# Set-up inside the fixed order, attention masks on GpSimd, new planner durations, a new copy order and dummy matmuls, in a fused attention and gated-convolution kernel

## The chip, the cores and the metric

The kernel runs on one core of a Trainium2 chip. The metric is the device time in microseconds (us) from the first to the last instruction of the run, as a median of several runs. A profiled run's *span* is a little shorter than the time quoted. A core has these engines: PE (matrix multiply, with weight loads shown as PEld), DVE (VectorE), ACT (ScalarE), POOL (GpSimd) and SP, which here issues most DMA transfers. SBUF and PSUM are the core's two on-chip memories; PE's results land in PSUM, and DVE or ACT copy them out to SBUF.

## The reference, cut to what matters

```python
# q, k, v: (8 batches, 8 heads, 576 positions, 64)
scores = (q @ k.T) / sqrt(64)
scores = where(abs(i - j) <= 32, scores, -1e9)       # window of 65 positions
x = softmax(scores) @ v                              # -> (8, 576, 512)
h = relu(x @ w_in)                                   # 512 -> 1024
gate = sigmoid(conv3(h))                             # 3 taps along the positions, per channel
out = (h * gate) @ w_out                             # 1024 -> 512
```

## The kernel before: the parts concerned

The kernel does not leave its order to a scheduler. Each piece of work is an `Op` with a believed duration on each engine that may run it. A list planner places all of them on a model of the engines and of PSUM's eight banks, and the instructions are emitted in the order of the planned starts. Every engine then runs its own list strictly in that order:

```python
def act(n): return ("ACT", 0.000833 * n + 0.068)          # believed us for n elements
def dve(n, mode=1): return ("DVE", n / (960.0 * mode) + 0.076)
...
with tc.manual_schedule():
    for op in plan.place():          # sorted by planned start
        op.run(op.eng)
```

The set-up (identity, band mask, zeroed paddings) stands ahead of that block and is placed by the framework. q and k come in as rows, 9 consecutive positions to a partition, and are transposed on PE, 4 + 4 + 1 position blocks at a time. The copy out of PSUM puts position `9*x + j` of head pair `g` in its place in `qT` or `kT`:

```python
o_ = T[:, :, ...].rearrange("p g (x j) -> p g x j", j=RP)       # RP = 9
def cp(e, o_=o_[:, :, :, j0:j1], a=a, n=n, sl=sl):              # n = j1 - j0 = 4 or 1
    copy(e, o_, ps(sl, 128 * a, 128 * (a + n)).rearrange(
        "p (j x g) -> p g x j", j=n, x=32))
on = dict([act(128 * n), dve(128 * n)])
```

The innermost index is `j`: four bf16 elements side by side in SBUF, then a step of nine. The masks multiply the exponentials on DVE:

```python
nc.vector.tensor_tensor(out=x, in0=x, in1=m__, op=ALU.mult)
```

The softmax here doesn't subtract the row's maximum and nothing guards it: scores larger than these inputs give would overflow.

## Time and profile before

The kernel before took 268.31 us (two runs, 267.78 to 268.85), and its profile spans 264.9 us. The main readings (busy time by stage, DVE's costly groups, the masks slowed beside POOL's casts, the waits of the set-up) are in the prediction below. Two more lines belong to the argument. The first is the engines' busy time in the whole span; the second, from the table by line and shape, is the group on ACT that copies `kT` (count, then busy us and mean ns of one, then idle time of the engine just before).

```profile
PE 226.6 (86%) x2515; PEld 137.7 (52%) x2538; DVE 201.0 (76%) x459; ACT 180.3 (68%) x367; POOL 77.0 (29%) x103
```

```profile
L247 ACT CAST kT<-ps_all 128x512 bf16<-128x512 f32 x29 | 20.2, 743 | 1.8 <-PE ps_all L451 1.4
```

In whole, the q and k copies of 512 elements are 64: 29 on DVE and 35 on ACT. The *own time* of an instruction is its end less the end of the one before it on its engine, so that the overlap of neighbours is taken off.

| before | us |
|---|---|
| time, median | 268.31 |
| 512-element q/k copy, own time (mean), DVE / ACT | 0.64 / 0.66 |
| 128-element q/k copy, own time (mean), DVE | 0.61 |

### The profile page before, as it was taken

To read this page: it belongs to the slowest core of one execution; us is meant where nothing else is said; L and a number is where in the kernel's file an instruction comes from. 1 tells how busy PE (TensorE), PEld (TensorE's weight loads), DVE (VectorE), ACT (ScalarE), POOL (GpSimd) and SP (SyncE) were. 2 spreads that over 40 slices of the span, in tenths; PEclk is the share of its full clock that TensorE was granted. 3 is DMA by queue.
4 is the path that set the end of the run, shared out by engine and by line. 5 is a ranking of instruction groups with operands and counts; after the bars stand their busy time and mean duration, and the time that the engine had idled before them with its cause. 6 is when DMAs were issued, how large, how long until landed. Compare 5 with 4: busy or idle time off the path is not lost.

```text
span 264.9 us, 6661 instructions
## 1 busy us (share of the span) xinstructions
PE 226.6 (86%) x2515; PEld 137.7 (52%) x2538; DVE 201.0 (76%) x459; ACT 180.3 (68%) x367; POOL 77.0 (29%) x103
## 2 busy tenths in 40 slices
PE   0337867995779998899999999999999999999973
PEld 0225757684367555455546555555464555555531
DVE  5452595369688999998888989899898998757650
ACT  2874877689357577768675858686867595666641
POOL 2677696319225506401224123231200000000000
PEclk9999997999799999999999999999999999999999
DMA  5999999999979898999999898952213131311113
GB/s 178 272 354 255 334 313 251 281 289 259 268 223 235 159 169 246 177 321 316 193 223 301 126 266 179 270 132 62 59 42 92 40 83 60 112 58 61 66 55 119
DMA packets 71123, 49.65 MB, mean 187 GB/s; under 512 B 54428, under 2 KB 54452, under 8 KB 71092
## 3 DMA queue, kind: packets, MB, share of 16 engines
q1 hardware_dynamic: 71056, 49.22, 74.3%
q8 instruction: 20, 0.33, 0.6%
q14 instruction: 11, 0.09, 0.1%
q10 hardware_dynamic: 36, 0.01, 0.0%
HBM read 32.52 MB, written 9.44 MB: 158 GB/s over the span
## 4 chain that ended last, share of the span: by engine, by line
PE 69%; DVE 17%; ACT 7%; issue 2%; DMA 2%; SPq 1%; POOL 1%; ACTq 0%; DVEq 0%
PE ps_all L680 24%; PE ps_all L752 22%; PE ps_all L710 12%; PE ps_all L549 5%; DVE attn L530 5%; DVE qT L253 4%; PE ps_all L451 3%; PE ps_all L502 3%; ACT kT L247 2%; ACT attn L515 2%; DMA kst<-in_k_dram 2%; DVE gT L732 2%; DVE xn L569 2%; DVE ps_all L725 2%; DVE kT L253 1%
## 5 line engine op out<-in xcount | busy, mean ns | idle before, releaser
L680 PE MATMUL ps_all<-xT,w_in_sb 128*128 128x385 bf16 (+4 forms) x448 | 81.1, 314 | 3.3 <-DVE xT L253 1.5
L752 PE MATMUL ps_all<-w_out_sb,gT 128*128 128x512 bf16 x265 | 66.8, 384 | 5.1 <-DVE gT L732 3.0
L732 DVE SCALAR_TENSOR_TENSOR gT<-ps_all,hT 128x384 bf16<-128x384 f32 (+3 forms) x112 | 55.1, 502 | 12.2 <-ACT ps_all L729 11.1
L729 ACT ACTIVATE ps_all<-ps_all 128x384 f32<-128x384 f32 (+3 forms) x112 | 49.2, 445 | 21.7 <-DVE ps_all L725 14.6
L725 DVE SCALAR_TENSOR_TENSOR ps_all<-hT,conv_w_sb,ps_all 128x384 f32<-128x384 bf16 x80 | 49.2, 624 | 15.9 <-PE ps_all L710 15.3
L696 ACT ACTIVATE hT<-ps_all 128x385 bf16<-128x385 f32 (+4 forms) x112 | 49.4, 452 | 14.8 <-PE ps_all L680 13.8
L680 PEld LDWEIGHTS <-w_in_sb 128*128 128x128 bf16 x448 | 41.2, 101 | 24.5 <-issue 2.3
L710 PE MATMUL ps_all<-hT,diag_w 128*128 128x384 bf16 (+3 forms) x256 | 51.0, 303 | 1.1 <-ACT hT L696 1.1
L752 PEld LDWEIGHTS <-gT 128*128 128x128 bf16 x288 | 27.8, 99 | 34.6 <-issue 6.0
L763 ACT COPY y<-ps_all 128x512 f32<-128x512 f32 x36 | 21.2, 588 | 30.7 <-PE ps_all L752 26.6
L249 POOL TENSOR_SCALAR ve<-vst 128x512 bf16<-128x512 f32 (+1 forms) x39 | 25.0, 652 | 47.1 <-PE ps_all L549 28.2
L515 ACT ACTIVATE attn<-ps_all 128x1024 bf16<-128x1024 f32 (+1 forms) x40 | 36.7, 943 | 2.1 <-PE ps_all L502 1.8
L530 DVE TENSOR_TENSOR attn<-attn,mask 128x1024 bf16<-128x1024 bf16 (+1 forms) x48 | 31.8, 682 | 5.1 <-ACT attn L515 4.9
L249 POOL TENSOR_SCALAR qn<-qst 128x1152 bf16<-128x1152 f32 (+1 forms) x18 | 19.5, 1091 | 48.1 <-issue 18.0
L253 DVE CAST qT<-ps_all 128x512 bf16<-128x512 f32 (+1 forms) x41 | 29.5, 736 | 5.3 <-PE ps_all L451 5.0
L569 DVE TENSOR_TENSOR xn<-ps_all,rec 128x256 bf16<-128x256 f32 (+1 forms) x64 | 30.4, 487 | 0.6
L710 PEld LDWEIGHTS <-diag_w 128*128 128x128 bf16 x256 | 21.8, 101 | 10.9 <-issue 1.3
L247 ACT CAST kT<-ps_all 128x512 bf16<-128x512 f32 (+1 forms) x32 | 22.7, 752 | 2.1 <-PE ps_all L451 1.4
L549 PEld LDWEIGHTS <-attn 128*64 128x64 bf16 x640 | 14.9, 112 | 17.5 <-issue 12.4
L549 PE MATMUL ps_all<-ve,attn 128*64 128x65 bf16 x384 | 20.2, 200 | 3.4 <-DVE attn L530 2.1
L451 PE MATMUL ps_all<-ident,qn 128*128 128x128 bf16 x144 | 15.4, 230 | 8.0 <-ACT qn L247 6.4
L249 POOL TENSOR_SCALAR kn<-kst 128x1152 bf16<-128x1152 f32 (+1 forms) x19 | 19.1, 1006 | 7.8 <-DMA kst<-in_k_dram 5.0
(47 smaller groups left out, 155.0 us busy)
## 6 DMA issues: line engine op xcount, KB each, us to landing
qst<-in_q_dram SPq DMA_DIRECT2D x32, 288.0 KB, 4.6
kst<-in_k_dram SPq DMA_DIRECT2D x32, 288.0 KB, 5.2
out_dram<-y SPq DMA_DIRECT2D x36, 256.0 KB, 2.3
vst<-in_v_dram SPq DMA_DIRECT2D x23, 256.0 KB, 6.1
vo<-ve SPq DMA_DIRECT2D x28, 130.0 KB, 4.5
vst<-in_v_dram SPq DMA_DIRECT2D x16, 192.0 KB, 5.7
wst<-in_moe_w_in_dram SPq DMA_DIRECT2D x2, 1024.0 KB, 8.5
wst<-in_moe_w_out_dram SPq DMA_DIRECT2D x2, 1024.0 KB, 9.2
```

The lines of the kernel that those rows point to most:

```text
L249: nc.gpsimd.tensor_scalar(out=out_, in0=in_, scalar1=1.0, scalar2=0.0, op0=ALU.mult, op1=ALU.add)
L253: nc.vector.tensor_copy(out_, in_)
L515: add(act(2 * w), t + 0.1, lambda e: nc.scalar.activation(at, ps(sl, 0, 1024).rearrange("p (e x) -> p e x", e=2)[:, :, 0:w], AF.Exp, bias= ...
L530: nc.vector.tensor_tensor(out=x, in0=x, in1=m__, op=ALU.mult)
L549: nc.tensor.matmul(ps(sl, (D + 1) * (n * h_ + x), (D + 1) * (n * h_ + x + 1), 64 * j, 64 * j + 64), attn[a][:, 512 * h_ + col:512 * h_ + c ...
L680: nc.tensor.matmul(ps(sl, 0, n), w_in_sb[:, kc, m * 128:(m + 1) * 128], x_[:, kc, a0:a1], start=(kc == 0), stop=(kc == KC - 1),)
L696: nc.scalar.activation(o_, i_, AF.Relu, bias=0.0, scale=0.5)
L710: nc.tensor.matmul(ps(sl, 0, no), diag_w[:, kk, m, :], hview(m, o0, o1, kk - 1), start=(kk == 0), stop=(kk == 2),)
L725: add(dve(no), tt + 0.1, lambda e, m=m, mid=mid, pv=pv: nc.vector.scalar_tensor_tensor(out=pv(), in0=mid, scalar=conv_w_sb[:, 1, m:m + 1], ...
L729: add(act(no), tt + 0.2, lambda e, sl=sl: nc.scalar.activation(ps(sl, 0, no), ps(sl, 0, no), AF.Tanh, bias=0.0, scale=1.0), writes=[sl], s ...
L732: add(dve(no), tt + 0.3, lambda e, m=m, mid=mid, i2=i2, pv=pv: nc.vector.scalar_tensor_tensor(out=gT[ig][:, m, o0:o1].rearrange("p (i x) - ...
L752: nc.tensor.matmul(ps(sl, 0, d_model), gT[ig][:, m, 128 * i:128 * i + 128], w_out_sb[:, m, :], start=(m == 0), stop=(m == MB - 1),)
```

## The change

The intent: keep the set-up where it delays nothing, relieve DVE of the masks of batches 2 to 7, give the planner the durations that the chip shows, make the copies of transposed q and k cheaper, and keep PE's clock up with dummy matmuls while it has no work. The diff, cut to its core:

```diff
-    nc.vector.memset(vst[0:PAD, 0, :, :], 0.0)            # set-up, ahead of the fixed order
-    ...
+    def setup():
+        nc.vector.memset(mask, 1.0)
+        make_identity(nc, ident)
+        ...                                              # masks first, paddings after
     with tc.manual_schedule():
-        for op in plan.place():
-            op.run(op.eng)
+        setup()
+        for _, _, run, arg in sorted(steps, key=lambda x: x[:2]):   # ops and dummies
+            run(arg)
...
-                add(dict([act(128), dve(128)]), 10.0 + m, diag, ...)
+                add(("DVE", 0.17), 10.0 + m, diag, ...)
...
-                o_ = T[...].rearrange("p g (x j) -> p g x j", j=RP)
-                    copy(e, o_[:, :, :, j0:j1], ps(...).rearrange("p (j x g) -> p g x j", j=n, x=32))
-                on = dict([act(128 * n), dve(128 * n)])
+                o_ = T[...].rearrange("p g (x j) -> p j g x", j=RP)
+                    if n == 1:
+                        copy(e, o_[:, j0], ps(...).rearrange("p (x g) -> p g x", x=32))
+                    copy(e, o_[:, j0:j1], ps(...).rearrange("p (j x g) -> p j g x", j=n, x=32))
+                on = dict([("ACT", 0.00095 * 128 * n + 0.1), ("DVE", 128 * n / 960.0 + 0.08)])
...
-        add(dve(2 * w, 2), t + 0.2, masks, ...)
+        add(("DVE", 2 * w / 1920.0 + 0.25) if b < 2 else ("POOL", 0.00188 * 2 * w + 0.155), t + 0.2, ...)
...
+    def warm(order):     # one 512-column matmul into bank 7 each 0.5 us of planned idle PE, 5 to 36 us
```

Further constants of the planner change too (latencies, DMA times, the time when each engine is first free).

More of the change, by code (lines that the diff above doesn't have):

```diff
@@ L13 @@
 ALU = mybir.AluOpType
+WARM = (5.0, 36.0)
 class Op:
@@ L72, in add @@
         return op
-    LAT = {"PE": 0.2, "ACT": 0.17, "DVE": 0.13, "POOL": 0.17}
+    LAT = {"PE": 0.22, "ACT": 0.16, "DVE": 0.13, "POOL": 0.2, "SP": 0.0, "ACTQ": 0.0}
+    EARLY = {"PE": 0.12, "ACT": 0.04, "DVE": 0.04, "POOL": 0.0, "SP": 0.0, "ACTQ": 0.0}
     def place(self):
@@ L87, in place @@
                 d.users.append(op)
-        free = dict.fromkeys(self.ENGINES, 0.8)
-        free["PE"] = 1.5
-        bank = [0.0] * self.banks
+        free = {"PE": 1.5, "ACT": 2.8, "DVE": 3.9, "POOL": 3.3, "SP": 0.8, "ACTQ": 0.8}
+        bank = [0.0] * (self.banks - 1) + [WARM[1]]
         dma_free = 0.0
@@ L116, in place @@
                 for e, d in op.on.items():
-                    s = max(r, free[e])
+                    s = max(r + self.EARLY[e] if r > 0.0 else r, free[e])
                     if best is None or s + d < best[1] - 1e-9:
@@ L288, in when @@
         return begin(b) + LB * (0.5 * s + 0.5 * x)
-    nc.vector.memset(vst[0:PAD, 0, :, :], 0.0)
-    nc.vector.memset(vst[128 - PAD:128, NBLK - 1, :, :], 0.0)
-    nc.scalar.dma_start(conv_w24, moe_conv_w.rearrange("k (m p) -> (k m) p", p=128))
-    make_identity(nc, ident)
-    nc.vector.tensor_copy(out=ident24, in_=ident[0:3 * MB, 0:3 * MB])
-    nc.vector.memset(mask, 1.0)
-    nc.gpsimd.affine_select(
-        out=mask, in_=mask, compare_op=ALU.is_ge, fill=0.0, base=0,
-        pattern=[[0, NT], [-1, 64]], channel_multiplier=1,
-    )
@@ L302 @@
-    nc.gpsimd.affine_select(
-        out=mask, in_=mask, compare_op=ALU.is_ge, fill=0.0, base=64,
-        pattern=[[0, NT], [1, 64]], channel_multiplier=-1,
-    )
-    nc.vector.memset(mask[0:PAD, 0, :], 0.0)
-    nc.vector.memset(mask[128 - PAD:128, NT - 1, :], 0.0)
-    for t_ in ve + vo[0:1]:
-        nc.vector.memset(t_[:, :, :, D], 1.0)
-    for t_ in kT:
-        nc.vector.memset(t_[:, :, 0:PAD], 0.0)
-        nc.vector.memset(t_[:, :, PAD + S:], 0.0)
-    nc.vector.memset(hT[0][:, :, 0], 0.0)
@@ L314 @@
-    nc.vector.memset(hT[1][:, :, HW + 1:HW + 3], 0.0)
-    nc.vector.memset(hT[2][:, :, CH + 1], 0.0)
+    def setup():
+        nc.vector.memset(mask, 1.0)
+        make_identity(nc, ident)
+        nc.gpsimd.affine_select(
+            out=mask, in_=mask, compare_op=ALU.is_ge, fill=0.0, base=0,
+            pattern=[[0, NT], [-1, 64]], channel_multiplier=1,
+        )
+        nc.gpsimd.affine_select(
+            out=mask, in_=mask, compare_op=ALU.is_ge, fill=0.0, base=64,
+            pattern=[[0, NT], [1, 64]], channel_multiplier=-1,
+        )
+        nc.vector.tensor_copy(out=ident24, in_=ident[0:3 * MB, 0:3 * MB])
+        nc.vector.memset(vst[0:PAD, 0, :, :], 0.0)
+        nc.vector.memset(vst[128 - PAD:128, NBLK - 1, :, :], 0.0)
+        for t_ in ve + vo[0:1]:
+            nc.vector.memset(t_[:, :, :, D], 1.0)
+        for t_ in kT:
+            nc.vector.memset(t_[:, :, 0:PAD], 0.0)
+            nc.vector.memset(t_[:, :, PAD + S:], 0.0)
+        nc.vector.memset(hT[0][:, :, 0], 0.0)
+        nc.vector.memset(hT[1][:, :, HW + 1:HW + 3], 0.0)
+        nc.vector.memset(hT[2][:, :, CH + 1], 0.0)
+        nc.vector.memset(mask[0:PAD, 0, :], 0.0)
+        nc.vector.memset(mask[128 - PAD:128, NT - 1, :], 0.0)
@@ L319, in conv_weights @@
     def conv_weights():
         s = Slot(1)
-        add(pe(24, 4), 6.0, lambda e: nc.tensor.matmul(
+        add(("ACTQ", 0.65), 0.0, lambda e: nc.scalar.dma_start(
+            conv_w24, moe_conv_w.rearrange("k (m p) -> (k m) p", p=128)
+        ), writes=["conv_w24"], dma=0.05)
+        add(pe(24, 20), 6.0, lambda e: nc.tensor.matmul(
             ps(s, 0, 3 * MB), conv_w24, ident24, start=True, stop=True
-        ), alloc=s, slots=[s], writes=[s])
+        ), alloc=s, slots=[s], reads=["conv_w24"], writes=[s])
@@ L330, in diag, with sp @@
                     o_, w_ = diag_w[:, kk, m, :], conv_w_sb[:, kk, m:m + 1]
-                    if e == "ACT":
-                        nc.scalar.activation(o_, ident, AF.Copy, bias=0.0, scale=w_)
-                    else:
-                        nc.vector.tensor_scalar(
-                            out=o_, in0=ident, scalar1=w_, scalar2=None, op0=ALU.mult
-                        )
-                add(dict([act(128), dve(128)]), 10.0 + m, diag, reads=["conv_w"], writes=[("diag", kk, m)])
-    def sp(cost=0.5):
+                    nc.vector.tensor_scalar(
+                        out=o_, in0=ident, scalar1=w_, scalar2=None, op0=ALU.mult
+                    )
+                add(("DVE", 0.17), 10.0 + m, diag, reads=["conv_w"], writes=[("diag", kk, m)])
+    def sp(cost=0.6):
         return ("SP", cost)
@@ L353, in load_qk @@
                 ),
-            ), writes=[("st", y, s, h_)], dma=0.77)
+            ), writes=[("st", y, s, h_)], dma=1.2 if (b, s) == (0, 0) else 0.85)
     def cast_qk(b, y, s, prio):
@@ L377, in load_v @@
         s0 = 128 * c - PAD + p0
-        add(sp(), prio, lambda e: nc.sync.dma_start(
+        add(sp(1.1), prio, lambda e: nc.sync.dma_start(
             vst[p0:p1, c, :, :], v[b, :, s0:s0 + p1 - p0, :].rearrange("h p d -> p h d")
-        ), writes=[("vst", c, x) for x in halves_of(p0, p1)], dma=0.01 * (p1 - p0))
+        ), writes=[("vst", c, x) for x in halves_of(p0, p1)], dma=0.0112 * (p1 - p0))
     def halves_of(p0, p1):
@@ L459, in transposes, with cp @@
                 T, off = (qT[i], 0) if y == 0 else (kT[i], PAD)
-                o_ = T[:, :, off + HS * s:off + HS * s + HS].rearrange("p g (x j) -> p g x j", j=RP)
-                def cp(e, o_=o_[:, :, :, j0:j1], a=a, n=n, sl=sl):
-                    copy(e, o_, ps(sl, 128 * a, 128 * (a + n)).rearrange(
-                        "p (j x g) -> p g x j", j=n, x=32))
-                on = dict([act(128 * n), dve(128 * n)])
+                o_ = T[:, :, off + HS * s:off + HS * s + HS].rearrange("p g (x j) -> p j g x", j=RP)
+                def cp(e, o_=o_, a=a, j0=j0, j1=j1, n=n, sl=sl):
+                    if n == 1:
+                        copy(e, o_[:, j0], ps(sl, 128 * a, 128 * (a + 1)).rearrange(
+                            "p (x g) -> p g x", x=32))
+                        return
+                    copy(e, o_[:, j0:j1], ps(sl, 128 * a, 128 * (a + n)).rearrange(
+                        "p (j x g) -> p j g x", j=n, x=32))
+                on = dict([("ACT", 0.00095 * 128 * n + 0.1), ("DVE", 128 * n / 960.0 + 0.08)])
                 if b > 1:
-                    on = dict([act(128 * n) if n_ % 2 else dve(128 * n)])
+                    e = "ACT" if n_ % 2 else "DVE"
+                    on = {e: on[e]}
                 add(on, t + 0.1, cp, reads=[sl], slots=[sl],
@@ L519, in scores @@
         if u is None:
-            m_ = mask[:, NT - 1].unsqueeze(1).broadcast_to([128, NP, 64])
-            parts = [(attn[a][:, 512 * h_:512 * h_ + w].rearrange("p (g x) -> p g x", g=NP), m_)
-                     for h_ in range(2)]
-        else:
-            m_ = mask[:, 4 * s:4 * s + 4].rearrange("p t x -> p (t x)")
-            parts = [(attn[a].rearrange("p (r x) -> p r x", r=4),
-                      m_.unsqueeze(1).broadcast_to([128, 4, 256]))]
-        def masks(e):
-            for x, m__ in parts:
-                nc.vector.tensor_tensor(out=x, in0=x, in1=m__, op=ALU.mult)
-        add(dve(2 * w, 2), t + 0.2, masks, reads=["mask"], writes=[("attn", a)], group=gr)
+            x_ = attn[a].rearrange("p (e x) -> p e x", e=2)[:, :, 0:w].rearrange("p e (g x) -> p e g x", g=NP)
+            m_ = mask[:, NT - 1].unsqueeze(1).unsqueeze(1).broadcast_to([128, 2, NP, 64])
+        else:
+            x_ = attn[a].rearrange("p (r x) -> p r x", r=4)
+            m_ = mask[:, 4 * s:4 * s + 4].rearrange("p t x -> p (t x)").unsqueeze(1).broadcast_to([128, 4, 256])
+        add(("DVE", 2 * w / 1920.0 + 0.25) if b < 2 else ("POOL", 0.00188 * 2 * w + 0.155), t + 0.2,
+            lambda e: ENG[e].tensor_tensor(out=x_, in0=x_, in1=m_, op=ALU.mult),
+            reads=["mask"], writes=[("attn", a)], group=gr)
     def values(b, s, g, t):
@@ L566, in values @@
         rv = rec[r][:, 0:2 * n].rearrange("p (c e) -> p c e", e=2)
-        add(dve(2 * n), t + 0.1, lambda e: nc.vector.reciprocal(rv, view()[:, :, :, D]),
+        add(("DVE", 0.1), t + 0.1, lambda e: nc.vector.reciprocal(rv, view()[:, :, :, D]),
             reads=[sl], writes=[("rec", r)], slots=[sl], group=gr)
@@ L724, in hidden @@
             if len(TAPS(c)) == 2:
-                add(dve(no), tt + 0.1, lambda e, m=m, mid=mid, pv=pv: nc.vector.scalar_tensor_tensor(
+                add(("DVE", no / 960.0 + 0.13), tt + 0.1, lambda e, m=m, mid=mid, pv=pv: nc.vector.scalar_tensor_tensor(
                     out=pv(), in0=mid, scalar=conv_w_sb[:, 1, m:m + 1], in1=pv(),
@@ L767, in project, with spin @@
             reads=[("y", r)], dma=0.8)
+    def warm(order):
+        def spin(n):
+            for _ in range(n):
+                nc.tensor.matmul(
+                    ps_all[:, 7 * 512:8 * 512], ident,
+                    mask.rearrange("p t x -> p (t x)")[:, 0:512], start=True, stop=True,
+                )
+        last, more = WARM[0], []
+        for op in order:
+            if op.eng != "PE":
+                continue
+            if op.start > WARM[1]:
+                break
+            t = last
+            while op.start - t > 0.5:
+                more.append((t + 0.05, spin))
+                t += 0.5
+            last = max(last, op.start + op.on["PE"])
+        return more
     conv_weights()
@@ L789 @@
             attention(c // 3 * 2 + 3)
+    order = plan.place()
+    steps = [(op.start, op.idx, op.run, op.eng) for op in order]
+    steps += [(t, -1, spin, 1) for t, spin in warm(order)]
     with tc.manual_schedule():
-        for op in plan.place():
-            op.run(op.eng)
+        setup()
+        for _, _, run, arg in sorted(steps, key=lambda x: x[:2]):
+            run(arg)
 _INS = ['q', 'k', 'v', 'moe_w_in', 'moe_conv_w', 'moe_w_out']
```

## The prediction

> **What bounds the kernel now.** I first cut the span where the load on the engines changes. This is the busy-by-stretch view of the kernel before (stretch, its length, then busy us and instruction count of each engine, granted clock, DMA share, GB/s):
>
> ```profile
> 0.00:75.00 75.00, 47.92 (x648) 36.39 (x650) 44.45 (x113) 50.76 (x110) 43.25 (x63) 0.95 1.03 274
> 75.00:222.00 147.00, 141.45 (x1672) 82.10 (x1691) 132.94 (x305) 105.96 (x208) 33.77 (x40) 1.00 0.76 176
> 222.00:264.90 42.90, 37.23 (x196) 19.22 (x197) 23.59 (x44) 23.56 (x50) 0.00 (x0) 0.99 0.22 76
> ```
>
> Columns are PE, PEld, DVE, ACT, POOL. In the middle stage PE looks 96% busy and DVE 90%, while POOL (GpSimd) has 113 us free. PE's busy time must not be taken at its word: a record includes the matmul's latency. So I took the typical spacing from one matmul's start to the next in the trace (216 ns for 512 columns, 164 for 385, 56 for 128, about 20 for the paired 64-column scores, 25 to 30 for the 65-column values) and multiplied by the counts. That PE work is 131 us of the 147 (89%), 21 us of the 30 between 45 and 75 us (69%), and 29.7 us of the 30 between 222 and 252 us (99%). Only the last stretch is at PE's own pace. PE waits in order for what DVE and ACT hand back, and DVE is the fullest of the two.
>
> What DVE spends it on, in the table by line and shape for all of the run (busy us, mean ns):
>
> ```profile
> L530 DVE TENSOR_TENSOR attn<-attn,mask 128x1024 bf16<-128x1024 bf16 x32 | 25.9, 815 | 4.5 <-ACT attn L515 4.3
> ...
> L253 DVE CAST qT<-ps_all 128x512 bf16<-128x512 f32 x26 | 18.6, 739 | 5.0 <-PE ps_all L451 4.7
> ...
> L253 DVE CAST kT<-ps_all 128x128 bf16<-128x128 f32 x13 | 11.9, 915 | 0.0
> ...
> L253 DVE CAST qT<-ps_all 128x128 bf16<-128x128 f32 x15 | 11.0, 732 | 0.3 <-PE ps_all L451 0.3
> ...
> L530 DVE TENSOR_TENSOR attn<-attn,mask 128x256 bf16<-128x256 bf16 x16 | 6.1, 418 | 0.7 <-ACT attn L515 0.7
> ```
>
> Two things stand out. A copy of 128 elements takes as long as one of 512. And the masks' mean hides a spread, which the timeline of DVE, then of POOL, shows at one place:
>
> ```profile
> 107.11 1.60 DVE L530 TENSOR_TENSOR attn<-attn,mask 128x1024 bf16<-128x1024 bf16 x1
> ...
> 109.25 1.49 DVE L530 TENSOR_TENSOR attn<-attn,mask 128x1024 bf16<-128x1024 bf16 x3
> ```
>
> ```profile
> 107.02 1.15 POOL L249 TENSOR_SCALAR kn<-kst 128x1152 bf16<-128x1152 f32 x1 [0.85 <-PE ps_all L502]
> 108.14 1.05 POOL L249 TENSOR_SCALAR ve<-vst 128x512 bf16<-128x512 f32 x1
> ```
>
> One mask beside POOL casts takes 1.60 us; three together soon after take 1.49. Counting each instruction's own time (its end less the end of the one before), masks average 0.63 us with POOL idle and 1.01 with POOL busy; POOL's wide casts go from 1.15 to about 1.45 when masks run. The two engines slow each other.
>
> The lead-in is bound otherwise. DMA share is 1.03 over the first 75 us, and 11.1 MB (batches 0 and 1, both weights) at about 280 GB/s is 40 us. Until some 43 us data arrives no sooner whatever the engines do. Beside that there are waits of the set-up's own making (the waits of DVE and PE) and a cold array (timeline of PE: sixteen 256-column matmuls in 3.57 us, 213 ns apart; four later ones in 0.60):
>
> ```profile
> DVE mask L306 <- POOL mask L302: 3.9, 1, 3.9
> ```
>
> ```profile
> PE ps_all L451 <- ACT qn L247: 6.4, 1, 6.4
> ```
>
> ```profile
> 22.91 3.57 PE L680 MATMUL ps_all<-xT,w_in_sb 128*128 128x256 bf16 x16 [0.88 <-DVE xT L253]
> ```
>
> ```profile
> 30.22 0.60 PE L680 MATMUL ps_all<-xT,w_in_sb 128*128 128x256 bf16 x4
> ```
>
> **What the Trainium skill says.** (1) "GPSIMD Engine Reference", section 1 "Specifications": GpSimd's SBUF interfaces are shared with VectorE, and contention arises with DVE instructions in a two-port mode or with two SBUF inputs. The trace agrees: masks have two SBUF inputs and go 0.63 to 1.01 us, while the gate product L732 and the tap L725, which have one PSUM input, do not slow (0.49 and 0.57 alone, 0.45 and 0.53 beside POOL). (2) The same page, section 3.1: about 2.6 cycles per element for a two-input GpSimd operation. At the 1.2 GHz it states, my estimate is 2.2 us for 1024 elements. The trace before has no such instruction; the planner's new constant gives 0.00188*1024+0.155 = 2.08. (3) "VectorE: DVE Perf Modes", tier table: a PSUM fp32 source runs at one element per cycle, 0.53 us for 512 at 0.96 GHz. The trace's 512 copies have own times of 0.62, so the new axis order can't gain much there. (4) "TensorE: Matmul & The Clock Gate", Part 1: the array idles at half clock until about 3.4 us of activity. The 213 against 108 ns agree; the granted-clock row of the page, at 9 or more there, does not show it. No page that I found says why a 128-element copy costs 0.6 us.
>
> **The change part by part.**
>
> *Masks to GpSimd.* Batches 2 to 7 have 4 wide masks and 2 narrow ones each: 24 x 0.76 + 12 x 0.35 = 22 us of own DVE time leave. POOL gets 24 x 2.08 + 6 x 1.12 (the two narrow ones merged, 512 elements) = 57 us. Per batch POOL then has 8.2 us of casts and 9.4 of masks, 17.6 in a batch period of some 25: about 70%. Each mask's latency grows by 1.3 us or so, but attention is planned a chunk ahead with six attn buffers. The mutual slowing goes too, apart from batches 0 and 1.
>
> *Single-block copies.* The pattern loses its innermost length of 1. I expect 0.2 us (128/0.96 plus a fixed part) in place of 0.60: 28 x 0.4 = 11 us off DVE, nearly 10 of it in batches 2 to 7. The 512 copies gain at most 0.03 on DVE and 0.07 on ACT.
>
> So DVE in the middle stage falls from 133 by about 20 (masks there) and 8 (20 small copies), to 105. At an occupancy of 90% that would need 117 us. PE's 131 us is then the bound, with ACT at about 104. With dependencies still leaving gaps, I put PE's share at 95% instead of 89%: 131/0.95 = 138, so **9 us** saved of a possible 16.
>
> *45 to 75 us.* PE waits there for copies and masks slowed by POOL (two took 2.17 us at 61 us). Batch 2's masks go to POOL at 2.08 each, which takes some of it back. Net **3 us**.
>
> *Set-up, diagonals, conv load.* The mask is made before the casts, so the 3.9 us DVE wait goes; the diagonals leave ACT (11 in 3.32 us ahead of the q cast) for DVE, where they own 0.17 each, 12 x 0.17 = 2 us more. First transposes can start about 2 us earlier, near 9. An ACT table load of 1.28 us may move in front of the first q cast.
>
> *Dummy matmuls.* Warm, the 16 matmuls at 22.9 us take 1.75 instead of 3.57, and the first attention some 2 us less: 3 to 4 us of PE time before 30 us. But DMA is the limit until 43 us, so of this and the set-up together I count **2.5 us**. Each dummy can delay a real matmul by 0.2 (warm) to 0.43 us; the eighth PSUM bank is withheld until 36 us.
>
> *Corrected durations.* They only reorder; I give them nothing by themselves, but they make the 95% believable.
>
> Sum: 9 + 3 + 2.5 = 14.5 us.
>
> **Rivals.** (A) *GpSimd becomes the bound or its latency shows*: at 2.2 to 2.5 us per mask and a cast of 1.2 in front, values wait and the in-order PE stalls. For it: late casts would also hold staging buffers and the loads. Against: POOL stays near 70%, and is unused after 190 us. Then perhaps 262 to 267. (B) *PE reaches its own pace*: 99% as after 222 us, so 14 us in the middle and more from 45 to 75: 245. Against: mixed stages have short, dependent groups. (C) *DMA takes over*: share 1.16 between 110 and 150 us. Against: loads end near 175 us, some 25 before batch 7 needs them. If it bound, 258 to 260. (D) *The lead-in gain is hidden* behind the loads: 256.
>
> **Range and chances.** 268.3 - 14.5 = 253.8. Weighing B at one in five and A or C at one in four, the range is 246 to 262. A gain of over 2% means below 262.9, a little above the range's top, so 0.88; within 2% 0.10; slower 0.02, since it needs a badly mistaken plan.
>
> **What would show it right or wrong.** Right: L530 on POOL near 2.1 us (24 wide, 6 narrow); the 128-element copies near 0.2 us of own time; masks left on DVE few; DVE busy near 168 us in all against 201 (24 of mask busy time and 11 of copies off, 2 of diagonals on), PE's middle stage some 9 us shorter, the 222-to-252 stretch unchanged. Wrong if PE waits for POOL attn come up in the waits by several us, if DVE's gain returns as PE or ACT waits, if the small copies stay at 0.6, or if the first projection still starts near 49 us and 45 to 75 keeps its length.

## The result, and the profile after

The changed kernel took **324.49 us** (two runs, 322.82 and 326.16): the ratio is 1.2094, with a 95% interval of 1.1806 to 1.2381. Ratios here and below are the mean time of one kernel's fast runs over that of the other's fast runs of the same rounds (each round times the kernel before as well), so not quite the ratio of the medians quoted. Its outputs are correct.

The busy time of the engines in the changed kernel:

```profile
PE 251.8 (78%) x2562; PEld 147.1 (45%) x2562; DVE 230.7 (71%) x433; ACT 233.6 (72%) x357; POOL 130.4 (40%) x131
```

POOL has the masks: 53 us more. But DVE, which lost them, has 30 us more and ACT 53. The table by line and shape names the cause:

```profile
L250 ACT CAST kT<-ps_all 128x512 bf16<-128x512 f32 x29 | 70.2, 2562 | 7.6 <-PE ps_all L454 7.4
L256 DVE CAST qT<-ps_all 128x512 bf16<-128x512 f32 x26 | 62.2, 2463 | 0.9 <-PE ps_all L454 0.9
L534 POOL TENSOR_TENSOR attn<-attn,mask 128x1024 bf16<-128x1024 bf16 x24 | 50.6, 2124 | 82.7 <-ACT attn L523 72.3 <-DVE rec L570 10.5
...
L256 DVE CAST kT<-ps_all 128x128 bf16<-128x128 f32 x13 | 12.1, 928 | 0.0
```

The reader is to compare three lines with those shown of before. The 512-element copies rose from 743 and 739 ns to 2562 and 2463. The 128-element copies did not move (915 to 928). The masks take on POOL what the planner believed: 2.1 us. With the overlaps taken off, the 64 copies cost 49 us more on DVE and 59 us more on ACT.

The busy-by-stretch view of the changed kernel (PE, PEld, DVE, ACT, POOL, clock, DMA share, GB/s) shows that the middle is thin rather than full:

```profile
75.00:222.00 147.00, 116.00 (x1291) 67.28 (x1289) 112.62 (x202) 104.23 (x153) 75.26 (x65) 0.87 0.63 164
```

In the same 147 us PE was busy for 141 us before and is for 116 now; no engine is full. The granted clock of PE is lower too, 0.87 against 1.00 before. One place in the timelines of DVE and then PE shows why:

```profile
78.62 4.65 DVE L256 CAST qT<-ps_all 128x512 bf16<-128x512 f32 x2
82.91 0.88 DVE L534 TENSOR_TENSOR attn<-attn,mask 128x1024 bf16<-128x1024 bf16 x1
83.72 0.33 DVE L735 SCALAR_TENSOR_TENSOR gT<-ps_all,hT 128x192 bf16<-128x192 f32 x1
```

```profile
77.18 1.04 PE L454 MATMUL ps_all<-ident,qn 128*128 128x128 bf16 x8
84.10 1.19 PE L454 MATMUL ps_all<-ident,kn 128*128 128x128 bf16 x8 [5.88 <-DVE gT L735]
```

Two copies that the plan booked at 0.61 us each hold DVE for 4.65 us. The gate product behind them is late, the PSUM bank that it frees is late, and PE, whose next instruction wants that bank, stands for 5.88 us. It may not take anything else out of turn. The waits of PE say the same in sum (total us, times, longest):

```profile
PE ps_all L713 <- ACT kT L250: 7.7, 6, 1.4
PE ps_all L510 <- ACT kT L250: 7.2, 3, 3.6
PE ps_all L454 <- DVE qT L256: 6.6, 5, 1.6
PE ps_all L454 <- DVE gT L735: 5.9, 1, 5.9
```

Three of the four name the copies of q and k. Before, the longest single waits of PE were the set-up's (6.4 and 3.7 us), and its largest wait for these copies, in sum, was this:

```profile
PE ps_all L502 <- ACT kT L247: 4.0, 3, 1.8
```

To see how far along each kernel is, I read from the timelines when the third output copy of a chunk starts. A chunk is two thirds of a batch; there are 12.

| kernel (one profile each) | chunk 1 | chunk 4 | chunk 9 | chunk 12 |
|---|---|---|---|---|
| before | 54.3 | 139.7 | 227.3 | 261.0 |
| changed | 59.1 | 174.1 | 287.6 | 320.7 |
| changed, old copy order | 45.8 | 127.4 | 217.3 | 250.4 |
| the same, masks on DVE | 46.1 | 131.5 | 218.8 | 252.0 |

### The profile page after: what moved, and what is told of

The parts are those of the page before. It is cut to its first block, busy times and chain, and to the rows that moved or that the text cites. A ratio compares the mean times of both kernels' runs of the same rounds, so it can differ in the third digit from the quotient of the medians.

```text
span 324.4 us, 6714 instructions
## 1 busy us (share of the span) xinstructions
PE 251.8 (78%) x2562; PEld 147.1 (45%) x2562; DVE 230.7 (71%) x433; ACT 233.6 (72%) x357; POOL 130.4 (40%) x131
## 4 chain that ended last, share of the span: by engine, by line
PE 47%; DVE 23%; ACT 19%; issue 8%; DMA 1%; SPq 0%; DVEq 0%; ACTq 0%
PE ps_all L755 17%; PE ps_all L683 13%; DVE qT L256 10%; ACT kT L250 10%; PE ps_all L713 8%; PE ps_all L510 3%; DVE ps_all L728 3%; PE ps_all L552 3%; DVE gT L735 3%; ACT attn L523 3%; ACT ps_all L732 2%; ACT qT L250 2%; DVE xn L572 2%; ACT hT L699 2%; DVE kT L256 2%
## 5 line engine op out<-in xcount | busy, mean ns | idle before, releaser
L534 POOL TENSOR_TENSOR attn<-attn,mask 128x1024 bf16<-128x1024 bf16 (+1 forms) x30 | 57.2, 1930 | 82.7 <-ACT attn L523 72.3
L683 PE MATMUL ps_all<-xT,w_in_sb 128*128 128x385 bf16 (+4 forms) x448 | 83.7, 320 | 5.1 <-DVE qT L256 2.8
L250 ACT CAST kT<-ps_all 128x512 bf16<-128x512 f32 (+1 forms) x32 | 72.4, 2425 | 7.6 <-PE ps_all L454 7.4
L755 PE MATMUL ps_all<-w_out_sb,gT 128*128 128x512 bf16 x288 | 73.0, 402 | 4.4 <-ACT kT L250 2.8
L256 DVE CAST qT<-ps_all 128x512 bf16<-128x512 f32 (+1 forms) x40 | 72.2, 1869 | 2.7 <-PE ps_all L454 2.7
L713 PE MATMUL ps_all<-hT,diag_w 128*128 128x384 bf16 (+3 forms) x256 | 53.5, 313 | 18.0 <-ACT kT L250 7.7
L732 ACT ACTIVATE ps_all<-ps_all 128x384 f32<-128x384 f32 (+3 forms) x112 | 52.7, 478 | 18.7 <-DVE ps_all L728 13.5
L699 ACT ACTIVATE hT<-ps_all 128x385 bf16<-128x385 f32 (+4 forms) x112 | 52.2, 478 | 18.3 <-PE ps_all L683 17.6
L454 PE MATMUL ps_all<-ident,kn 128*128 128x128 bf16 x144 | 16.8, 240 | 10.4 <-DVE gT L735 5.9
L510 PE MATMUL ps_all<-qT,kT 64*128 64x64 bf16 x576 | 16.4, 204 | 10.0 <-ACT kT L250 7.2
```

Source lines behind the costliest of these rows:

```text
L250: nc.scalar.copy(out=out_, in_=in_)
L256: nc.vector.tensor_copy(out_, in_)
L534: lambda e: ENG[e].tensor_tensor(out=x_, in0=x_, in1=m_, op=ALU.mult),
L683: nc.tensor.matmul(ps(sl, 0, n), w_in_sb[:, kc, m * 128:(m + 1) * 128], x_[:, kc, a0:a1], start=(kc == 0), stop=(kc == KC - 1),)
L699: nc.scalar.activation(o_, i_, AF.Relu, bias=0.0, scale=0.5)
L713: nc.tensor.matmul(ps(sl, 0, no), diag_w[:, kk, m, :], hview(m, o0, o1, kk - 1), start=(kk == 0), stop=(kk == 2),)
```

## The experiments

Twelve kernels ran, all correct. **Theory S**: the new order of the q and k copies is the loss. **Rival M**: the loss is in the masks on POOL, the dummies or the new plan. **Rival P**, on the mechanism: it is the order of reading PSUM that costs, and not the scattered writing.

### One part undone: the old copy order

```diff
-                o_ = T[...].rearrange("p g (x j) -> p j g x", j=RP)      # and the two copies
+                o_ = T[...].rearrange("p g (x j) -> p g x j", j=RP)
```

> The changed kernel with one thing undone: the q/k transposes' copies out of PSUM walk in the old order again (four adjacent destination elements innermost). The planner's numbers stay those of the changed kernel. Theory S (the new order of the copies costs about 1.7 us on each of 64 copies, and that is the whole loss): the 512-element copies go back to about 0.65 us, and the time falls from 324 to 245-260 us, below before. Rival M (the loss lies in the masks on GpSimd, the dummy matmuls or the new plan): the copies get short but the time stays over 280 us.

Measured: 256.66 us, ratio 0.9645 (0.9595 to 0.9696) to before. The lines by shape:

```profile
L250 ACT CAST kT<-ps_all 128x512 bf16<-128x512 f32 x29 | 20.8, 750 | 4.1 <-DVE attn L530 2.8 <-PE ps_all L454 1.0
L256 DVE CAST qT<-ps_all 128x512 bf16<-128x512 f32 x26 | 18.6, 727 | 1.3 <-PE ps_all L454 1.3
L256 DVE CAST kT<-ps_all 128x128 bf16<-128x128 f32 x13 | 12.1, 929 | 0.0
```

Only the order of the copies differs from the changed kernel, plan and all else being equal, and 0.245 of the time of before (1.2094 less 0.9645, some 66 us) goes with it. What is left of the change is a gain of 3.5%.

### One part alone: the new copy order in the kernel before

```diff
-                o_ = T[...].rearrange("p g (x j) -> p g x j", j=RP)
+                o_ = T[...].rearrange("p g (x j) -> p j g x", j=RP)      # and the two copies
```

> The kernel before with only the new order of the q/k copies, and its old planner numbers. Theory S: the copies take 2.3 us and the time rises to 300-330 us with masks on the Vector engine, no dummies and the old plan. Rival M: under 280 us.

Measured: 332.16 us, ratio 1.2484 (1.2427 to 1.2540), with masks on DVE, no dummies and the old plan. Rival M falls: the copies alone make the loss, and need nothing else of the change.

### The copies measured by themselves

Copies of PSUM were appended to the kernel before, each alone on its engine, three times.

```diff
+    c(out=W0[:, 0:512], in_=P0)                                                                        # L804
+    c(out=W0[:, 0:512].rearrange("p (g x) -> p g x", g=4), in_=P0.rearrange("p (x g) -> p g x", g=4))  # L805
+    c(out=W0[...].rearrange("p (x r) -> p x r", r=2)[:, :, 0], in_=P0)                                 # L806
+    c(out=W0[...].rearrange("p (x r) -> p x r", r=3)[:, :, 0], in_=P0)                                 # L807
+    c(out=Q4[:, :, :, 0:4], in_=P0.rearrange("p (j x g) -> p g x j", j=4, x=32))         # L811, old order
+    c(out=Q4.rearrange("p g x j -> p j g x")[:, 0:4], in_=P0.rearrange("p (j x g) -> p j g x", j=4, x=32))  # L812, new
```

> The kernel before with 30 copies of a PSUM bank on each of the Vector and Scalar engines appended after its work (384 and 512 elements, outputs unused). Theory S (cost by the number of runs of adjacent destination elements, about 4.5 ns each): contiguous destination about 0.6 us even where the source is read with a stride of 4; destination stride 2 or 3 in bf16 2.3 us; runs of two 1.15 us; runs of four 0.6 us; stride 3 in fp32 open. Rival P (the order in which PSUM is read costs): the strided source into a contiguous destination takes 2.3 us, the contiguous source into a strided destination 0.6 us.

By line and shape, ACT (DVE differs by about 0.1 us at most). Each bench is a single profiled run of unknown state; its three repeats agree within 0.02 us, except for the first after a pause:

```profile
L812 ACT CAST qT<-ps_all 128x512 bf16<-128x512 f32 x3 | 7.2, 2387 | 0.1
...
L807 ACT CAST wst<-ps_all 128x512 bf16<-128x512 f32 x3 | 3.0, 1007 | 0.1
...
L811 ACT CAST qT<-ps_all 128x512 bf16<-128x512 f32 x3 | 2.2, 727 | 0.0
L806 ACT CAST wst<-ps_all 128x512 bf16<-128x512 f32 x3 | 2.2, 726 | 0.1
...
L804 ACT CAST wst<-ps_all 128x512 bf16<-128x512 f32 x3 | 1.8, 588 | 0.0
...
L805 ACT CAST wst<-ps_all 128x512 bf16<-128x512 f32 x3 | 1.8, 585 | 0.1
```

Rival P falls with the last two lines: a source read four apart into a contiguous destination takes 585 ns, against 588 from a contiguous source (by own time at most 0.1 us more, where rival P needs 1.7). The new order takes 2387 ns with nothing beside it. But theory S had the strides 2 and 3 at 2.3 us, and they took 0.73 and 1.01. A price per run of adjacent elements was too simple, so a second bench swept the stride (256 elements, bf16: L803 stride 3, L804 4, L806 8, L807 9, L809 16; fp32: L810 stride 4; and 128 runs every ninth element: L812 of one, L815 of four).

> The kernel before with copies of 256 elements from PSUM appended, bf16 at destination strides 2, 3, 4, 6, 8, 9, 12, 16, fp32 at 4 and 8, and runs of 1, 2, 3, 4 adjacent elements every 9 (128 runs). Theory L (each pass over a stretch of destination costs by its bytes, some 17 to 20 ns per 64 bytes partly written): stride 9 1.2 us, 12 1.6, 16 2.2 us, and runs of 1 to 4 all about 0.6 us. Theory E (each separate element costs up to 4.6 ns, whatever the stride from about 9 on): strides 9, 12 and 16 all 1.2 us, runs of 1 to 4 all 0.6 us too.

```profile
L806 ACT CAST wst<-ps_all 128x256 bf16<-128x256 f32 x3 | 3.9, 1289 | 0.1
...
L807 ACT CAST wst<-ps_all 128x256 bf16<-128x256 f32 x3 | 3.8, 1277 | 0.2
...
L809 ACT CAST wst<-ps_all 128x256 bf16<-128x256 f32 x3 | 3.7, 1227 | 0.2
...
L812 ACT CAST qT<-ps_all 128x128 bf16<-128x128 f32 x3 | 2.3, 768 | 0.0
L804 ACT CAST wst<-ps_all 128x256 bf16<-128x256 f32 x3 | 2.2, 724 | 0.1
...
L815 ACT CAST qT<-ps_all 128x512 bf16<-128x512 f32 x3 | 2.2, 720 | 0.1
...
L810 ACT COPY wst<-ps_all 128x256 f32<-128x256 f32 x3 | 1.8, 607 | 0.1
L803 ACT CAST wst<-ps_all 128x256 bf16<-128x256 f32 x3 | 1.8, 584 | 0.1
```

For bf16 the price rises with the stride to 1.29 us at 8 elements, which is 16 bytes, and then stands still: strides 9, 12 and 16 took 1.28, 1.28 and 1.23. That is theory E, and theory L, which wanted 2.2 us at stride 16, falls. A bf16 element that lands 16 bytes or more from the last costs about 5 ns (1.29 us / 256). 128 runs of one or of four cost 0.56 and 0.72 us of own time (0.77 and 0.72 with overlap). So the old order's copy pays mainly for 128 landings and the new one for 512: at 4.7 ns each (0.60 us / 128), 2.4 us. The same arithmetic says why the single-block copy is slow in both kernels: 128 elements, 128 landings.

Why a landing costs this is not shown. The Trainium skill, "SBUF — State Buffer", section "Specifications (TRN2)", has lines of 16 bytes, full bandwidth only with at least two hits per line, and a penalty for each cross to a new line. The bf16 runs agree in that the price stops rising at 16 bytes. But they don't agree with full bandwidth at two hits per line: stride 4 puts two bf16 elements on a line and took 0.72 us, against 0.33 of own time at stride 2. And an fp32 element that lands 16 bytes from the last (L810) cost about half as much, 0.61 us / 256 = 2.4 ns, so the line is not the whole reason. The price is measured here; its cause stays open.

### Price against surprise: the slow copies, known to the planner

```diff
-                on = dict([("ACT", 0.00095 * 128 * n + 0.1), ("DVE", 128 * n / 960.0 + 0.08)])
+                on = {"ACT": 2.35 if n > 1 else 0.59, "DVE": 2.32 if n > 1 else 0.6}
```

> The changed kernel with the new copy order kept and the planner told its real price (2.32 us on the Vector engine, 2.35 on the Scalar engine for four blocks; 0.60 and 0.59 for one) instead of 0.61, 0.59 and 0.21, 0.22. If most of the loss is the work itself (64 copies, 1.7 us more each): the time stays near 310-325 us. If most of it is that the fixed order believes 0.6 us and PE waits in order for copies that are late: 280-300 us.

Measured: 281.21 us, ratio 1.0504 (1.0465 to 1.0542). The copies are as slow as in the changed kernel (2.34 us of own time on either engine). What is another follows from the durations alone: the order, and the engine of three copies (32 on each, in place of 29 and 35). With that, 0.159 of before (43 us) comes back. More than half of the loss was the plan's surprise and not the copies' work. With it the clock comes back as well: between 75 and 222 us PE is granted 0.99 here, against 0.87 in the changed kernel. How many of the 43 us are due to the waits alone and how many to the lower clock beside them was not separated.

### Fast copies, known to the planner

```diff
+                on = {"ACT": 0.67 if n > 1 else 0.59, "DVE": 0.63 if n > 1 else 0.6}     # old copy order
```

> The run with the old copy order, the planner told what these copies measure (0.63 and 0.60 us on the Vector engine, 0.67 and 0.59 on the Scalar engine, for four blocks and for one) in place of 0.61 and 0.21, and 0.59 and 0.22. If a plan that believes 0.4 us too little per single-block copy costs waits: 1 to 4 us faster than with the old copy order, near 0.955. Else within 1 us.

Measured: 253.58 us, ratio 0.9500 (0.9449 to 0.9551), and once more, in other rounds:

> The best run so far again (old copy order, real copy times in the plan, masks on GpSimd, set-up in the fixed order, dummies): 0.945 to 0.955 of before.

Measured: 253.07 us, ratio 0.9460 (0.9414 to 0.9506). This is the best version: it beats before by 5% and the changed kernel by over a fifth. Against the slow copies that the planner knows (1.0504, same rounds) the work of the copies is 0.104 of before, 28 us. Against 0.9645 with the wrong durations (0.9595 to 0.9696), 0.9500 and 0.9460 are lower by 1.5 to 1.9%, and neither interval overlaps with that one; but the runs are of other rounds.

### Masks back on DVE

```diff
-        add(("DVE", ...) if b < 2 else ("POOL", 0.00188 * 2 * w + 0.155), t + 0.2, ...)
+        add(("DVE", 2 * w / 1920.0 + 0.25), t + 0.2, ...)
```

> As the run with the old copy order, and the masks of batches 2 to 7 back on the Vector engine (the two narrow ones still merged). If moving the masks is worth what the prediction said of the middle stage, this is 5 to 12 us slower than the run with the old copy order alone. If GpSimd's longer latency eats the gain, the two are within 2 us.

Measured: 258.21 us, ratio 0.9705 (0.9653 to 0.9756), against 0.9645 with masks on POOL. Then the pair with the real copy times:

> Old copy order, real copy times in the plan, masks of batches 2 to 7 on the Vector engine. Against the same with the masks on GpSimd (sent along again): the prediction's 9 us would make this 3.5% slower; if the middle stage is bound by PE anyway and the masks' move is worth about what the first pair showed, 0.3 to 1.5% slower.

Measured: 255.00 us, ratio 0.9491 (0.9449 to 0.9534), against 0.9460. Both pairs point the same way, by 0.3 to 0.6%, and in both the intervals overlap. The move of the masks reads as 1 to 2 us; whether it is more than nothing these runs don't settle.

### Dummies and set-up

```diff
-    steps += [(t, -1, spin, 1) for t, spin in warm(order)]
+    steps += [(t, -1, spin, 1) for t, spin in []]
```

> The run with the old copy order, less the 24 dummy matmuls; the plan is the same, the eighth PSUM bank still withheld. Prediction's reasoning (loads set the pace until 43 us, so a warm array is worth little there): within 1.5 us of the run with the old copy order (0.9645 of before). Rival (the lead-in's 8.5 us come from the warm clock): 4 us or more slower, about 0.98.

Measured: 258.44 us, ratio 0.9685 (0.9633 to 0.9736), against 0.9645 with dummies: 1 to 2 us, intervals overlapping, in other rounds. By the measure of the table, chunk 1 stands at 49.3 in its profile against 45.8. Next, from this kernel, the set-up moved out of the fixed order:

```diff
+    setup()
     with tc.manual_schedule():
-        setup()
```

> The run without dummies, and the set-up emitted ahead of the fixed order again, where the framework places it by its own priorities. If the set-up's place is worth the 3.9 us wait that it removes: 2 to 5 us slower than the run without dummies. If the lead-in is bound by loads or by the new plan alone: within 1 us of it.

Measured: 265.12 us, ratio 0.9967 (0.9909 to 1.0024): 2.8% slower than with the set-up inside, and clear of noise. The waits of DVE, then of PE, with the set-up outside, and PE's for the same copies with it inside:

```profile
DVE mask L317 <- POOL mask L302: 5.0, 1, 5.0
```

```profile
PE ps_all L454 <- DVE qT L256: 7.8, 1, 7.8
```

```profile
PE ps_all L454 <- ACT kn L250: 2.5, 1, 2.5
```

The framework put half of the mask behind a v cast that waits for its load. DVE then waits 5.0 us at the mask's padding, with twelve diagonals and then a q copy behind it, and PE stands 7.8 us for that copy. Inside, the first k transposes wait only for their own cast.

Last, the set-up moved alone in the kernel before:

```diff
     with tc.manual_schedule():
+        setup()          # new order of set-up, the rest as before
```

> The kernel before with nothing changed but the set-up: in the new order and inside the fixed order. The pair with and without the set-up in the fixed order gave 4 to 7 us; if that holds on its own: 0.975 to 0.985 of before. The diagonals still stand on the Scalar engine before the first q cast here, so less is possible; under 1 us would say that the set-up is worth something only together with them.

Measured: 266.41 us, ratio 0.9919 (0.9865 to 0.9972): some 2 us, less than the expected 1.5 to 2.5%. Here the diagonals still hold ACT ahead of the first q casts. That they are what hides the rest was not tested.

## Why the prediction was wrong, point by point

**The step that failed** is the part "Single-block copies": "I expect 0.2 us (128/0.96 plus a fixed part) in place of 0.60", and "The 512 copies gain at most 0.03 on DVE and 0.07 on ACT". I took the small copy's price for the price of an innermost length of 1. It was the price of 128 separate landings, and the new order made 512 of them out of 128 in each large copy. The small ones stayed at 0.6, which the prediction had named as a sign of being wrong, and the large ones went from 0.64 to 2.3. The clue was in the page before: 128 landings cost 0.6 us with one element in each and with four. I said that no page explained it, and had not looked at the memory's own page, which at least says that lines count.

**The second part of that failure** is that no rival let a believed duration be wrong; only the 0.02 for "slower" spoke of a badly mistaken plan. The prediction gave the corrected durations nothing by themselves. A wrong one turned a loss of 28 us, had the plan known it, into one of some 66, because the order is fixed.

**The masks**: the cost was right (2.08 us said, 2.10 of own time measured; 24 wide and 6 narrow; POOL never full), the worth was not. Of the "9 us" for masks and small copies together, the small copies gave nothing and the masks 1 to 2. Where it went is argued from the table of chunks, with one profile each, and not shown by an experiment. From chunk 4 to 9 the kernel before already took 87.6 us for five chunks, and the one with the old copy order 89.9 (masks on POOL) or 87.3 (on DVE). At my spacings a chunk needs about 16.8 us of PE by the program's count of matmuls, and 17.5 were taken. The prediction counted only the matmuls in the trace, which lacks 23 of the 288 of the output projection. With those of 75 to 222 us put back (17, at 216 ns), the 131 us of PE work are about 135, and the slack is 12 us in place of 16. It is larger before chunk 4 (PE work some 88% of the time from 75 to 139.7 us) than after (some 94% up to 222). So I had averaged one stage over two regimes. Two more sums are slightly off, without effect: the masks of the middle stage are 18.7 us of busy time and not 20, and the loads are 11.3 MB and not 11.1. Rival A (latency shows, 262 to 267) did not come.

**The lead-in** was undervalued: "2.5 us" for set-up and dummies; chunk 1 stands 8.5 us earlier with the old copy order (54.3 to 45.8), which is most of the final 10.6 us. The planner's other constants changed too, so not all of that need be set-up and dummies. The set-up's place is 2.8% in the one comparison that isolates it among the other changes. My "DMA is the limit until 43 us" fits batch 1, whose last load lands at 41.6 us before and 42.1 with the old copy order. But chunk 1 needs batch 0 and the weights, whose last cast on POOL begins at 37.6 and 37.3 us. Rival D falls with it.

**What held**: the ACT table load did move in front of the first q cast, and cost nothing there (it ran from 1.4 to 2.7 us, while ACT waited until 4.1 for the data). No load stands out among PE's waits with the old copy order: the longest waits of PE for a DMA are 2.5 us, for the convolution's weights at the start, and 1.0. And the rest of the change, without the copy order, lands at 256.66 us, inside the range of 246 to 262, for partly wrong reasons.

What stays open: how much of the masks' and the dummies' one or two us each is real, why the set-up alone gives less than it does among the others, what the lower clock cost, and why a scattered bf16 element costs twice an fp32 one.

## What to carry to other kernels

Count the separate landings of a bf16 copy's destination, not its elements: an access order that looks tidier can quadruple them. Where the order of instructions is fixed by a model, a wrong duration can cost more than the work itself (here some 38 of 66 us), so measure each changed instruction by itself before the plan is built on it. And before crediting relief of a busy engine, check that the stage is not already at the pace of another, chunk by chunk rather than in one average.

## What the Trainium skill lacked or had wrong

- "SBUF — State Buffer", "Specifications (TRN2)": it has the 16-byte lines and says that each cross to a new line pays a penalty, but no price for a scattered bf16 write of VectorE or ScalarE. Measured for 256 elements out of PSUM: about 0.33 us of own time at stride 2, 0.72 at 4, 1.29 at 8, and flat from there (1.28 at 9, 1.23 at 16), some 5 ns per landing and the same on both engines; fp32 took half (0.61 us at stride 4, 0.62 at 8). Full bandwidth at two hits per line does not hold for these writes: stride 4 puts two bf16 elements on a line and took over twice the time of stride 2. Already stride 3 costs: 0.58 us.
- "VectorE: DVE Perf Modes", tier table: read alone, one element per cycle from PSUM fp32 gives the prediction's 0.53 us for 512 elements, which is an estimate; with a scattered destination it took 2.4. The table has no word on the destination's stride.
- "GPSIMD Engine Reference", section 3.1: 2.6 cycles per element gave my estimate of 2.2 us for a 1024-element two-input operation; measured 2.10 on bf16. The estimate is 5% high; the page's own figure is for fp32, and no run here has that.
- No page has a size for this pair, a mask on DVE (two SBUF inputs) beside a cast on POOL. Measured in the kernel before: 0.63 us for the mask alone, 1.01 beside POOL's casts.
